# Moving one direct load of x ahead of the second group of output stores in a fused Fourier mixing and ELU kernel

## The chip, the cores and the metric

The kernel runs on one core of one Trainium2 chip. The metric is the device time of one execution in microseconds, as the median of several runs; lower is better. A profile of one execution on the same core gives the start and the duration of every instruction, the waits between engines, and the time at which DMA transfers land.

## What is computed

The input x has shape (8, 3008, 256) in float32. Each of the 8 batches goes through a two-dimensional Fourier transform, over the 3008 positions and over the 256 channels, of which the real part is kept. Each of the 24064 rows then goes through two matrices with an ELU between them:

```python
X = np.fft.fft(x, axis=1)
X = np.fft.fft(X, axis=2).real
x = X.reshape(B * S, D)
h = x @ w_in                                  # (24064, 256) @ (256, 2048)
g = np.where(h > 0.0, h, np.exp(np.minimum(h, 0.0)) - 1.0)
out = g @ w_out                               # (24064, 2048) @ (2048, 256)
```

## The kernel before

**The steady work.** Symmetry of the transform lets the kernel work on half of the positions, 8 x 1504 columns. They are cut into tiles of 256 columns, and each tile is passed over in 8 steps of two blocks of hidden units. One step is a fixed pattern on four engines. TensorE (PE) multiplies the transformed columns with the folded first matrix into the bank H (`mm_P`, `mm_Q`). VectorE (DVE) and ScalarE (ACT) make two ELU blocks of it, of which `g_plus` and `g_minus` are the last operations. GpSimd (POOL) makes four sums of blocks, in the order `sum_1`, `sum_3`, `sum_2`, `sum_4`; all of them pass through the helper at L548 and appear in the profile as `G<-G`. PE then multiplies the blocks and sums with the second matrix: `mm_X1` (L1310), `mm_X2` (L1318) and `mm_X3` (L1325). The third product of `mm_X1`, `pB<-G,WT` in the profile, reads the block that `sum_2` has written. All matmuls pass through the helper at L539.

**The output.** After a tile's 8 steps its result is combined, turned and stored. `turn_u` (L1368) transposes one half on VectorE and calls `store` twice; `turn_v` (L1389), one step later, does the same for the other half. `store` (L1398) issues its DMAs on SyncE's queue (SP) at L1424, most of them of 32 KB or less in runs of 128 bytes. Each of the two halves gives 16 or 20 stores where the change is made, and both halves go out of one buffer `ot`, of which there are two.

**The next batch.** Between these steps the kernel prepares the transform of the next batch. For batches b = 2 to 7, `load_quarter(b, j, far)` (L276) loads row tile j = 0 to 3 in two halves, near (far = 0) and far (far = 1), both into the tile `xl`j (`xq` in the profile). Tiles that are read against the order of the rows use a gather: an indirect DMA that GpSimd issues at L288. The others are direct loads on SyncE's queue at L301; a direct far half consists of two pieces, 80 rows (320 KB) and 14 rows (56 KB). For the far half, tiles 1 and 2 are direct, and 0 and 3 are gathers. `mirror_sum` (L686) then adds tile 1 to tile 0 and tile 2 to tile 3 on GpSimd, in eight parts that alternate between the two pairs, one part for each step; the first part of a pair also adds a four-element edge. `half_sum`, `channel_fold` and `channel_edge` continue from there. A far half may only be loaded when the near half in the same tile has been read to the end.

**What sets the order.** The order on PE, VectorE, ScalarE and GpSimd is written out by hand: every operation is put on a list with a due time (`at`; `rel` for the batch preparation, counted in steps of T = 4.8 from r0 = 48 b - 70), the list is sorted (L1916), and compute operations are pinned to that order. The direct loads and the stores on SyncE's queue are not pinned. The scheduler places them, so that their place in the finished program need not be their place on the list. Waits are added for data, for buffers, and for the semaphore that a DMA signals with; SyncE's DMAs take eight such semaphores (lanes) in turn, and a DMA waits until the one that had its lane before has landed.

On the list, `turn_u` of a tile stands at dt 4.2 of the step with number 3 (counted modulo 8) and `turn_v` at dt 4.2 of step 4. For a batch, step r0 + 26 is such a step 4.

Of the kernel before, what the change touches and what calls it, by code (L numbers as in the profile page):

```python
# [162 lines left out]
def kernel(  # L163
# [977 lines left out]
    def spread_ext(b, kodd):  # L1141
        for sl, a, z in ring_cut(b * HALF + kodd * RUN, RUN, False):
            a, z = a + kodd * RUN, z + kodd * RUN
            nc.sync.dma_start(
                out=Rb[:, sl],
                in_=r128_dr[b : b + 1, a:z].to_broadcast([128, z - a]),
            )
            nc.sync.dma_start(out=Ir[127:128, sl], in_=r128_dr[b : b + 1, a:z])
# [367 lines left out]
    def at(t, fn):  # L1516
        events.append((t, len(events), fn))
# [220 lines left out]
    def safe(col):  # L1738

        return 8 * ((col - 1 - RING) // TW) + 8 if col > RING else 0  # L1740
# [86 lines left out]
    def at_quarter(step, b, ri, kodd, finish, join):  # L1827
        box = []

        def d():  # L1830
            if not box:
                box.append(Quarter(ri, b, kodd, state["Q", ri, kodd, b]))
            return box[0]

        def half(par):
            d().ps = bank("H")
            d().mms(par, d().ps)

        at(step * T + 4.75, lambda: half(0))
        at((step + 1) * T + 0.9, lambda: d().copy())  # L1840
        at((step + 1) * T + 1.0, lambda: d().unfold())
        at((step + 2) * T + 4.75, lambda: half(1))
        if kodd:
            at(finish * T + 4.26, lambda: d().finish())
            at((step + 3) * T + 0.9, lambda: d().copy_odd())
            at((step + 3) * T + 1.0, lambda: d().unfold_odd())
        assert join + 1 >= safe(b * HALF + (kodd + 1) * RUN)
        t = join * T + (4.25 if kodd else 1.01)
        at(t, lambda: d().plus())
        at(t + 0.001, lambda: d().minus())  # L1850

    for b in range(2, NB):
        s0 = (b - 1) * steps_b
        r0 = 48 * b - 70

        def rel(step, dt, fn, *key):
            at((r0 + step) * T + dt, lambda: fn(*key))

        for far, rows in (
            (0, ((0, 2, 0.2), (1, 2, 1.3), (3, 3, 0.2), (2, 3, 1.3))),  # L1860
            (1, ((0, 27, 1.3), (1, 25, 0.2), (3, 28, 1.3), (2, 27, 0.2))),
        ):
            for j, n, dt in rows:
                rel(n, dt, load_quarter, b, j, far)
        rel(5, 3.0, quarter_row, b)
        for far, start in ((0, 6), (1, 30)):
            for n in range(8):
                rel(start + n, 1.3, mirror_sum, (0, 3)[n % 2], far, n // 2)
        for step, *key in (
            (13, 0, 0, 0), (20, 1, 0, 0), (21, 0, 0, 1), (22, 1, 0, 1),  # L1870
            (35, 0, 1, 0), (36, 1, 1, 0), (37, 1, 1, 1), (38, 0, 1, 1),
        ):
            rel(step, 4.25, half_sum, *key)
        for step, *key in (
            (14, 0, 0, 0), (21, 1, 0, 0), (23, 0, 0, 1), (25, 1, 0, 1),
            (38, 0, 1, 0), (40, 1, 1, 0), (42, 1, 1, 1), (44, 0, 1, 1),
        ):
            for ri in range(2):
                rel(step + ri, 1.3, channel_fold, ri, *key)
            kodd, far, h = key  # L1880
            if h:
                rel(step, 4.0, channel_edge, kodd, far)
        for n in range(4):
            ri, m = divmod(n, 2)
            rel(46 + n, 1.3, quarter_pairs, b, ri, 0, 1 + m)
        for n, step in enumerate((43, 44, 45, 46, 51, 53)):
            ri, m = divmod(n, 3)
            rel(step, 4.25, quarter_pairs, b, ri, 1, (2, 1, 3)[m])
        for step, ri, kodd, finish, join in (
            (51, 0, 0, 0, 54),  # L1890
            (56, 1, 0, 0, 59),
            (59, 0, 1, 60, 75),
            (64, 1, 1, 66, 76),
        ):
            at_quarter(r0 + step, b, ri, kodd, r0 + finish, r0 + join)
        for kodd in range(2):
            step = s0 + (28, 38)[kodd]
            assert step >= safe(b * HALF + (kodd + 1) * RUN)
            at(step * T + 1.0, lambda b=b, kodd=kodd: spread_ext(b, kodd))
# [48 lines left out]
```

## Time and profile before

| what | value |
|---|---|
| median of three timed runs | 1926.92 us (1926.02 to 1929.34) |
| the profiled execution's own time | 1925.81 us |
| its span, first to last instruction | 1924.0 us |
| granted TensorE clock | 1.000 |
| out_dram<-ot stores of 32 KB on SP | 496 |
| xq direct loads on SP: near 384 KB, far 320 KB, far 56 KB | 12 of each |
| xq gathers on GpSimd | 24, median 7.9 us from issue to landing |

Times of single instructions are microseconds from the start of the span. In the views of the profile a row of a timeline gives start, duration, engine, line, operation, tile written and tiles read, the number of merged instructions, and in brackets the engine's idle time before it with what ended that. A row of the table of waits gives the engine and line that waited, what ended the wait, the total in us, how often, and the longest. A row of the chain of waits gives start, duration, and the engine and tile that the time belongs to. A name ending in q (SPq) is the engine's queue of waits and DMA issues, which the profile doesn't count as busy.

### The profile page before, as it was taken

What the parts mean: (1) busy time and instruction counts of PE and PEld (TensorE: products, weight loads), DVE (VectorE), ACT (ScalarE), POOL (GpSimd) and SP (SyncE); (2) the same over time, 40 slices, a digit from 0 to 9 for tenths busy, and PEclk for the clock granted to TensorE, in tenths of its full rate; (3) what the DMA queues carried; (4) which work ended last, traced back from release to release, by engine and by line L of the source; (5) the groups of instructions that cost most, each with busy time, mean ns of one, the idle gap of its engine ahead of it and who ended that gap; (6) DMA issues with size and microseconds to landing.
All of it is one profiled execution on the core that took longest, in us unless ns stands there. A gap on an engine that the chain in (4) does not pass through costs nothing.

```text
span 1924.0 us, 27630 instructions
## 1 busy us (share of the span) xinstructions
PE 1910.7 (99%) x9008; PEld 1653.7 (86%) x9008; DVE 1436.7 (75%) x2714; ACT 872.7 (45%) x1710; POOL 1357.3 (71%) x1843
## 2 busy tenths in 40 slices
PE   9999999999999999999999999999999999999999
PEld 6788788888888888888888888888888888888887
DVE  8876767877777777777777777777777777667666
ACT  5644444444444444444444444444444444444443
POOL 4788857786677766787667776677766777556565
PEclk9999999999999999999999999999999999999999
DMA  8146212111021110211101111022110210100101
GB/s 337 44 34 51 45 31 55 37 23 33 12 45 36 29 31 12 51 29 32 26 19 45 33 27 27 12 52 42 26 20 12 52 23 15 17 12 13 21 11 23
DMA packets 271073, 71.88 MB, mean 37 GB/s; under 512 B 256815, under 2 KB 257731, under 8 KB 270929
## 3 DMA queue, kind: packets, MB, share of 16 engines
q1 hardware_dynamic: 257296, 57.34, 15.1%
q0 software_dynamic: 11456, 12.52, 2.2%
q8 instruction: 71, 1.16, 0.3%
q14 instruction: 74, 0.60, 0.1%
q10 hardware_dynamic: 2176, 0.26, 0.1%
HBM read 45.20 MB, written 24.80 MB: 36 GB/s over the span
## 4 chain that ended last, share of the span: by engine, by line
PE 86%; DMA 4%; POOL 3%; SPq 2%; DVE 2%; issue 1%; ACT 0%; POOLq 0%; DVEq 0%
PE H L539 34%; PE pB L539 15%; PE pC L539 15%; PE pD L539 15%; PE pA L539 7%; DMA out_dram<-ot 4%; SPq L1424 2%; POOL G L548 2%; POOL WT L548 1%; DMA xq<-in_x_dram 1%; DVE G L1223 0%; DMA xl<-in_x_dram,ix 0%; POOL e L548 0%; DVE E L1193 0%; DVE e L636 0%
## 5 line engine op out<-in xcount | busy, mean ns | idle before, releaser
L548 POOL TENSOR_TENSOR G<-G 128x256 f32<-128x256 f32 x1440 | 1046.6, 736 | 496.0 <-DVE G L1223 337.2
L551 ACT ACTIVATE G<-H 128x512 f32<-128x512 f32 x376 | 224.6, 597 | 941.3 <-DVE G L1207 936.5
L1193 DVE SCALAR_TENSOR_TENSOR E<-Rb,wex,H 128x256 f32<-128x256 f32 x752 | 327.7, 477 | 380.7 <-PE H L539 375.7
L539 PE MATMUL H<-Ir,Ws 128*128 128x256 f32 x1504 | 387.0, 380 | 2.0 <-DVE E L1193 2.0
L539 PE MATMUL H<-Rr,Wc 128*128 128x256 f32 x1504 | 387.9, 380 | 0.8 <-DVE Ir L545 0.8
L539 PE MATMUL pC<-G,WT 128*128 128x256 f32 x1440 | 369.5, 379 | 0.0
L539 PEld LDWEIGHTS H<-Ir,Ws 128*128 128x128 f32 x1504 | 278.8, 189 | 50.1 <-DVE E L1193 5.1
L539 PEld LDWEIGHTS H<-Rr,Wc 128*128 128x128 f32 x1504 | 282.1, 190 | 44.1 <-issue 2.2
L539 PEld LDWEIGHTS pC<-G,WT 128*128 128x128 f32 x1440 | 273.6, 190 | 37.2
L1207 DVE SCALAR_TENSOR_TENSOR G<-E,H 128x512 f32<-128x512 f32 x376 | 256.8, 683 | 49.5 <-POOL G L548 14.7
L1223 DVE SCALAR_TENSOR_TENSOR G<-G,H 128x512 f32<-128x512 f32 x376 | 255.8, 680 | 37.5 <-ACT G L551 37.5
L1223 DVE SCALAR_TENSOR_TENSOR G<-M,G 128x512 f32<-128x512 f32 x376 | 256.7, 683 | 0.4 <-ACT M L551 0.4
L551 ACT ACTIVATE G<-G 128x512 f32<-128x512 f32 x376 | 233.4, 621 | 0.0
L539 PE MATMUL pD<-G,w 128*128 128x256 f32 x784 | 229.3, 379 | 0.0
L539 PE MATMUL pA<-G,w 128*128 128x256 f32 x784 | 229.3, 379 | 0.0
L539 PE MATMUL pB<-G,w 128*128 128x256 f32 x784 | 229.3, 379 | 0.0
L551 ACT ACTIVATE M<-G 128x512 f32<-128x512 f32 x376 | 224.0, 596 | 3.1 <-DVE G L1207 3.1
L551 ACT ACTIVATE M<-M 128x512 f32<-128x512 f32 x376 | 221.2, 588 | 0.1
L539 PE MATMUL pB<-G,WT 128*128 128x256 f32 x720 | 215.0, 380 | 4.7 <-POOL G L548 4.6
L539 PE MATMUL pD<-G,WT 128*128 128x256 f32 x720 | 214.1, 379 | 0.0
L539 PEld LDWEIGHTS pA<-G,w 128*128 128x128 f32 x784 | 148.9, 190 | 20.5
L539 PEld LDWEIGHTS pD<-G,w 128*128 128x128 f32 x784 | 149.0, 190 | 20.3
(178 smaller groups left out, 1539.8 us busy)
## 6 DMA issues: line engine op xcount, KB each, us to landing
out_dram<-ot SPq DMA_DIRECT2D x496, 32.0 KB
xq<-in_x_dram SPq DMA_DIRECT2D x12, 384.0 KB
out_dram<-ot SPq DMA_DIRECT2D x256, 2.0 KB
xq<-in_x_dram SPq DMA_DIRECT2D x12, 320.0 KB
Rb<-r SPq DMA_DIRECT2D x10, 376.0 KB
raw<-in_moe_w_in_dram SPq DMA_DIRECT2D x7, 512.0 KB
MC<-dft_mats SPq DMA_DIRECT2D x3, 943.5 KB
xl<-in_x_dram SPq DMA_DIRECT2D x4, 512.0 KB
```

Of the source, the lines that this page charges most:

```text
L539: nc.tensor.matmul(out_, lhsT=lhsT, rhs=rhs, start=start, stop=stop, skip_group_check=True)
L548: pin(nc.gpsimd.tensor_tensor(out=o, in0=a, in1=b, op=op))
L551: pin(nc.scalar.activation(out=o, in_=i, func=func, **kw))
L1193: nc.vector.scalar_tensor_tensor(out=S.E[:, c], in0=Rb[:, cols(i)], scalar=wex[:, f : f + 1], in1=S.H[:, c], op0=ALU.mult, op1=ALU.add,)
L1207: nc.vector.scalar_tensor_tensor(out=two(S.G[:, 0:512])[:, :, ::-1], in0=two(S.E), scalar=2.0, in1=two(S.H), op0=ALU.mult, op1=ALU.subtract,)
L1223: nc.vector.scalar_tensor_tensor(out=o, in0=e, scalar=-1.0, in1=h, op0=ALU.add, op1=ALU.max)
L1424: queue.dma_start(out=bass.AP(tensor=out.tensor, offset=out.offset + r0 * ND + half * 128 + 32 * g, ap=[[2 * ND, w], [64 * ND, nb], [1, 32 ...
```

## The change

The due time of the direct load of row tile 2's far half changes from step r0 + 27, dt 0.2, to step r0 + 26, dt 3.0. On the list it then stands between `turn_u` and `turn_v` of the output tile instead of after both. Everything else is as before.

```diff
         for far, rows in (
             (0, ((0, 2, 0.2), (1, 2, 1.3), (3, 3, 0.2), (2, 3, 1.3))),
-            (1, ((0, 27, 1.3), (1, 25, 0.2), (3, 28, 1.3), (2, 27, 0.2))),
+            (1, ((0, 27, 1.3), (1, 25, 0.2), (3, 28, 1.3), (2, 26, 3.0))),
         ):
             for j, n, dt in rows:
                 rel(n, dt, load_quarter, b, j, far)
```

In each row of four the entries are the row tile j, the step and dt.

## The prediction

> **What bounds the kernel now.** I read the page's table of engines first. TensorE (PE) is busy for practically the whole span; no other engine comes near.
>
> ```profile
> PE 1910.7 (99%) x9008; PEld 1653.7 (86%) x9008; DVE 1436.7 (75%) x2714; ACT 872.7 (45%) x1710; POOL 1357.3 (71%) x1843
> ```
>
> So only a change that closes a hole in PE's row can shorten the run, and there are 1924.0 - 1910.7 = 13.3 us of holes. Next the table of waits (engine, line, what it waited for: total us, times, longest), for two rows:
>
> ```profile
> POOL xq L548 <- DMA xq<-in_x_dram: 17.4, 6, 4.4
> ...
> PE pB L539 <- POOL G L548: 4.6, 6, 1.8
> ```
>
> GpSimd (POOL) waits six times, once per batch b = 2 to 7, for a load of x; PE waits six times for GpSimd. The chain of waits that ended last joins the two. These are its steps in the second of those batches (b = 3); the columns are start, us, and who:
>
> ```profile
> 556.66 9.28 DMA out_dram<-ot
> 565.96 5.48 DMA out_dram<-ot
> 575.63 1.95 DMA xq<-in_x_dram
> 578.63 1.37 POOL G L548 x2
> ```
>
> Output stores hold up a load of x, the load holds up GpSimd, and GpSimd ends PE's wait. The same four steps return at 795.92, 1033.76, 1271.50 and 1508.99, and not in b = 2. Now each engine's own timeline at that place. SyncE's queue (SP):
>
> ```profile
> 541.49 9.03 SPq L301 DMA_DIRECT2D xq<-in_x_dram  x3
> 550.63 24.95 SPq L1424 DMA_DIRECT2D out_dram<-ot  x40
> 575.63 0.33 SPq L301 DMA_DIRECT2D xq<-in_x_dram  x1
> 576.05 0.35 SPq L1144 DMA_DIRECT2D Rb<-r  x1
> ```
>
> Of the four pieces of direct load (two each for row tiles 1 and 2), three are issued by 550.5. The last, the 14-row piece of tile 2 (56 KB), stands behind all 40 stores of one output tile: 20 of turn_u, 20 of turn_v. GpSimd:
>
> ```profile
> 568.62 0.89 POOL L548 TENSOR_TENSOR xq<-xq,xq 94x255 f32<-94x255 f32 x2
> 570.31 3.03 POOL L548 TENSOR_TENSOR G<-G 128x256 f32<-128x256 f32 x4 [0.79 <-DVE G L1223]
> 577.73 0.90 POOL L548 TENSOR_TENSOR xq<-xq,xq 94x255 f32<-94x255 f32 x2 [4.40 <-DMA xq<-in_x_dram]
> 578.57 3.03 POOL L548 TENSOR_TENSOR G<-G 128x256 f32<-128x256 f32 x4
> ```
>
> The second mirror_sum of the far half could have begun at 577.73 - 4.40 = 573.33. The four G<-G behind it are sum_1, sum_3, sum_2 and sum_4; sum_2, the third, ends near 580.8. PE:
>
> ```profile
> 578.42 0.59 PE L539 MATMUL pB<-G,w 128*128 128x256 f32 x2
> 580.85 0.70 PE L539 MATMUL pB<-G,WT 128*128 128x256 f32 x2 [1.83 <-POOL G L548]
> 581.38 0.81 PE L539 MATMUL H<-Ir,Ws 128*128 128x256 f32 x3
> ```
>
> The matmul that stalls is the third product of mm_X1, which reads the block that sum_2 writes.
>
> **What the Trainium skill says.** (1) "DMA: Bandwidth & Descriptors", section "Anatomy of one DMA": DMA engines do not wait on semaphores; the issuing sequencer does, before dispatch. The trace agrees: SP issues nothing between 560.8 and 562.9, nor between 563.2 and 566.0, while an earlier store on its semaphore lane is still landing (lanes are used eight in turn, so a ninth DMA waits for the first). (2) The same page, "Queues, rings and completion order": on each DMA engine the descriptors of one issuing queue are consumed in ring order. The trace agrees as far as it can: the load that follows the drained stores lands in 1.95 us, while stores issued into the backlog need 4.7 to 9.7 us. (3) The same page, "Issuing engines are not separate DMA queues": SP's transfers and GpSimd's gathers run on the same 16 engines and interleave. The two gathers of b = 3 take 12.2 and 11.5 us beside the stores, against a median of 7.9 for all 24.
>
> **The change, part by part.** It removes and adds no instruction. The two programs as built have the same order on PE, VectorE, ScalarE and GpSimd. On SP the 80-row piece stays where it was, ahead of all the stores; only the 14-row piece moves, from behind turn_v's stores to between turn_u's and turn_v's: 20 stores sooner (16 in b = 2). The waits on readers of the tile stay with the 80-row piece; the 14-row piece keeps one wait, for its semaphore lane. The lanes of the stores it passes shift by one. The gathers' place on GpSimd's queue is unchanged, and so is what follows on SP (the Rb and Ir spreads at 576.05).
>
> When does the 14-row piece land now? It takes the place and the lane of turn_v's first store, so I use that store's times. In b = 3 it was issued at 560.50, and its lane was taken again at 569.12, so it had landed by then. In the other batches: b = 2 321.94 and 329.77; b = 4 799.20 and 807.01; b = 5 1036.71 and 1045.31; b = 6 1273.56 and 1281.96; b = 7 1510.97 and 1518.79. GpSimd's earliest need (start of the waiting mirror_sum less its wait) is 336.65, 573.33, 812.09, 1049.91, 1287.17 and 1525.08. The margins are 6.9, 4.2, 5.1, 4.6, 5.2 and 6.3 us. The wait for this piece should disappear in every batch.
>
> What is late next? The same mirror_sum waits for the gather of tile 3. The gathers land at 334.59, 571.20, 809.50, 1046.84, 1284.54 and 1522.49, which is 2.1 to 3.1 us ahead of need. There is also a cover between GpSimd and PE: GpSimd waited 4.40, 3.48, 2.92, 3.16 and 3.18 us in b = 3 to 7, and PE stood for 1.83, 0.92, 0.34, 0.60 and 0.61. The difference is 2.56 to 2.58 us each time. A GpSimd wait under 2.57 us costs PE nothing, and b = 2 confirms it: 0.27 us of wait and no stall. So the gather could come some 4.7 us later than now before PE noticed.
>
> Could the moved piece delay a gather so much? Its 14 packets of 4 KB take about 0.26 us each, and they go to 14 engines. That puts 0 to 0.3 us ahead of other traffic, against 4.7 us of cover: cost nothing. turn_v's stores go out one place later, by 0.3 us (the issue time of one such DMA) up to the 2.4 us that SP may wait for the next lane (562.91 - 560.50), but the sum of issues ahead of the Rb spread is unchanged, and it was issued on VectorE's release at 576.11. The output buffer that these stores read is wanted again two tiles, or 16 steps of about 4.75 us, later. That slack of over 70 us hides it.
>
> What is a stall worth? PE's start-to-start distance is what is lost, and it is more than the idle time printed, because a matmul's modelled end lies after the next one's start. From the start of mm_X1's pB<-G,w to the start of the next H<-Ir,Ws, b = 2, which has no stall, takes 337.86 - 336.99 = 0.87 us. In b = 3 it takes 581.38 - 578.42 = 2.96, so 2.09 is lost. In b = 4 to 7 the distances are 2.06, 1.47, 1.73 and 1.74, so 1.19, 0.60, 0.86 and 0.87. The sum is 2.09 + 1.19 + 0.60 + 0.86 + 0.87 = 5.61 us. The printed idle times alone give 1.83 + 0.92 + 0.34 + 0.60 + 0.61 = 4.30 us: that is the lower bound. Between 337 and 1525 the table of stages shows PE busy to the full in every stretch without such a stall, so no other wait is in line behind them, and b = 2 shows the next 48 steps running on without one. I take 5.6.
>
> The span falls from 1924.0 to 1918.4. The profiled execution took 1925.81 us, 1.81 more than its span; the same on top gives 1920.2. The three timed runs have a median of 1926.92, 1.1 above the profiled one. On that median: 1926.92 - 5.6 = 1921.3.
>
> **The rivals.** *Part of it* (chance 0.08): the piece lands later than turn_v's first store did, since a 4 KB packet in a ring of 128 B ones need not behave the same, or the gather moves later, so that some wait beyond the cover stays. For it: SP's backlog is worst just there. Against: over 4 us of margin and 2.57 of cover. With half of the loss left, 1926.9 - 2.8 = 1924.1.
>
> *Nothing* (0.05): the wait closes and PE loses the time to another engine later, for instance because VectorE used the stall to catch up. Against: VectorE is at 75%, and after the stall-free b = 2 PE is full from 337 to 574. It would give 1926.9.
>
> *Slower* (0.04): the gather becomes the last to land and is pushed back by the earlier piece. It must come later than the 14-row piece did before (577.58, 815.41, 1052.67, 1290.17, 1528.10), so by 5.6 to 6.4 us; from there every us costs one per batch. If gathers were 8 us later they would end 2.4 to 3.4 us past need plus cover in each of six batches, 17.5 us in all: 1926.9 + 17.5 - 5.6 = 1938.8. For it: they share the engines. Against: 0.3 us of traffic.
>
> **How the numbers follow.** The full gain has 0.83. A measurement here can tell about 0.2%, or 3.85 us, from no change, so the bound is 1923.07. Faster: 0.82 of the full gain and 0.03 of the partial one; slower 0.04; the rest is the same. The range: downwards 5.6 plus 0.4 (a small PE loss between 1295 and 1525 which might go too) below the fastest run, 1926.02, hence 1919.5 with a little for scatter; upwards past the lower bound (1922.6) to the partial case at 1924.2.
>
> **What would show it.** Right: GpSimd's row of waits on xq falls from 17.4 us to under 2; the row PE pB on POOL G loses its five stalls; the chain passes no out_dram or xq step; SP issues a single xq load between two groups of 20 stores near 560. Wrong: the mirror_sum still waits near its present length, with a gather as the one that ended it; or PE shows a new releaser within some steps of the old stall.

## The result, and the profile after

The changed kernel takes 1921.05 us (median of six runs, 1920.68 to 1921.22), beside 1927.99 us for the kernel before (six runs, 1926.02 to 1931.73). The ratio is 0.9962, with a 95% interval of 0.9949 to 0.9975: faster by 0.25 to 0.5%. The forecast was 1921.3, in a range of 1919.5 to 1924.2. The profiled execution of the changed kernel took 1921.02 us with a span of 1919.1, against 1925.81 and 1924.0.

First SyncE's queue in batch b = 3, at the place shown in the prediction:

```profile
542.04 9.04 SPq L301 DMA_DIRECT2D xq<-in_x_dram  x3
551.20 9.03 SPq L1424 DMA_DIRECT2D out_dram<-ot  x20
561.00 0.34 SPq L301 DMA_DIRECT2D xq<-in_x_dram  x1
563.54 13.05 SPq L1424 DMA_DIRECT2D out_dram<-ot  x20
576.69 0.35 SPq L1144 DMA_DIRECT2D Rb<-r  x1
```

The single load, the 14-row piece, now stands between two groups of 20 stores. It was issued at 561.00 instead of 575.63, and the last signal of its landing came at 567.47 (its lane was taken again at 568.74). The second group of stores begins later (563.54; it was 560.50), and the Rb spread only 0.64 us later, both counted from the start of the span. Of each, 0.5 us was there before this place was reached: the same steps at 436 already run that much later in this execution.

GpSimd at the same place:

```profile
569.17 0.89 POOL L548 TENSOR_TENSOR xq<-xq,xq 94x255 f32<-94x255 f32 x2
570.88 3.02 POOL L548 TENSOR_TENSOR G<-G 128x256 f32<-128x256 f32 x4 [0.82 <-DVE G L1223]
573.86 0.89 POOL L548 TENSOR_TENSOR xq<-xq,xq 94x255 f32<-94x255 f32 x2
576.21 3.03 POOL L548 TENSOR_TENSOR G<-G 128x256 f32<-128x256 f32 x4 [1.46 <-PE H L539]
```

The second mirror_sum follows the sums without a bracket, that is, without a wait. GpSimd then waits for the ordinary step of the pattern. PE:

```profile
578.99 0.59 PE L539 MATMUL pB<-G,w 128*128 128x256 f32 x2
579.42 0.59 PE L539 MATMUL pB<-G,WT 128*128 128x256 f32 x2
579.86 1.03 PE L539 MATMUL H<-Ir,Ws 128*128 128x256 f32 x4
```

From pB<-G,w to H<-Ir,Ws it is 579.86 - 578.99 = 0.87 us, the undisturbed distance; it was 2.96. The table of waits has no row of GpSimd on the direct load any more (it was 17.4 us, 6 times), and of the row of PE pB on POOL G (4.6 us, 6 times) this is left:

```profile
PE pB L539 <- POOL G L548: 0.3, 1, 0.3
```

That one wait, at 226.6, lies ahead of these batches and was there before too (226.2); the five stalls are gone. The chain that ended last has no store and no load of xq in it. By engines it reads, before and after:

```profile
PE 86%; DMA 4%; POOL 3%; SPq 2%; DVE 2%; issue 1%; ACT 0%; POOLq 0%; DVEq 0%
```

```profile
PE 96%; DVE 1%; POOL 1%; ACT 0%; DMA 0%; issue 0%; DVEq 0%; POOLq 0%
```

### The profile page after: what moved, and what is told of

It reads as the page before. It is cut to its first block, busy times and chain, and to the rows that moved or that the text cites. A ratio compares the mean times of both kernels' runs of the same rounds, so it can differ in the third digit from the quotient of the medians.

```text
span 1919.1 us, 27636 instructions
## 1 busy us (share of the span) xinstructions
PE 1909.2 (99%) x9008; PEld 1653.4 (86%) x9008; DVE 1436.9 (75%) x2714; ACT 872.3 (45%) x1710; POOL 1356.9 (71%) x1843
## 4 chain that ended last, share of the span: by engine, by line
PE 96%; DVE 1%; POOL 1%; ACT 0%; DMA 0%; issue 0%; DVEq 0%; POOLq 0%
PE H L539 38%; PE pB L539 17%; PE pC L539 17%; PE pD L539 16%; PE pA L539 9%; POOL WT L548 1%; DMA xl<-in_x_dram,ix 0%; POOL w L548 0%; DVE e L636 0%; ACT G L551 0%; DVE pow L407 0%; DVE o L636 0%; DVE E L1193 0%; DVE G L1223 0%; DVE G L1207 0%
## 5 line engine op out<-in xcount | busy, mean ns | idle before, releaser
L548 POOL TENSOR_TENSOR G<-G 128x256 f32<-128x256 f32 x1440 | 1045.6, 735 | 508.6 <-DVE G L1223 341.9
```

Source lines behind the costliest of these rows:

```text
L548: pin(nc.gpsimd.tensor_tensor(out=o, in0=a, in1=b, op=op))
```

## The experiments

The theory: the 14-row piece lands late because of its place behind the stores, GpSimd waits for it, and what goes beyond 2.57 us of that wait becomes a stall of PE. The main rivals: every store ahead of the load costs its share; the due time or the kind of load is what counts; the gather is the next bound. "Before" and "after" are the two kernels of the change. Each run was timed beside the kernel before, on the same chip.

| run | median us | ratio to before, 95% interval | GpSimd waits for xq, us (b = 2 to 7) | PE idle in the stalls, us |
|---|---|---|---|---|
| before, first profile | 1926.92 | | 0.27, 4.40, 3.48, 2.92, 3.16, 3.18 | 0, 1.83, 0.92, 0.34, 0.60, 0.61 |
| e0, before again | 1927.68 | 1.0002 (0.9993 to 1.001) | 0.54, 4.56, 4.11, 3.51, 3.49, 3.09 | 0, 1.99, 1.54, 0.96, 0.92, 0.53 |
| after | 1921.05 | 0.9962 (0.9949 to 0.9975) | none | none |
| e1, big piece last | 1937.67 | 1.0051 (1.0037 to 1.0065) | 0.62, 5.26, 5.25, 4.88, 5.48, 3.89 | 0, 2.68, 2.67, 2.30, 2.90, 1.31 |
| e2, behind 8 stores of turn_v | 1921.12 | 0.9967 (0.9954 to 0.9979) | none | none |
| e3, behind 12 | 1920.55 | 0.9964 (0.9951 to 0.9978) | 0, 0, 0.63, 0.44, 0.32, 0 | none |
| e4, one piece | 1921.66 | 0.9968 (0.9955 to 0.998) | none | none |
| e5, gather one step later | 1921.53 | 0.997 (0.9959 to 0.9981) | 1.87, 2.43, 2.83, 2.38, 2.15, 2.14 | 0, 0, 0.27, 0, 0, 0 |
| e6, gather two steps later | 1963.53 | 1.0184 (1.017 to 1.0198) | 7.55, 6.16, 6.31, 5.78, 6.12, 7.57 | 5.75, 4.36, 4.51, 4.00, 4.34, 5.86 |

**The kernel before, once more (e0).** No edit.

> The kernel before, unchanged, for a second profile and more times. My theory (the small load lands late, GpSimd waits, and what exceeds 2.57 us of that wait becomes a PE stall): five PE stalls again at pB<-G,WT, each equal to GpSimd's wait on xq less 2.57 us; if this execution is slower than the first profiled one (1925.81 us), the stalls are longer by just that, since the landing of the load is what varies. Rival (the runs of before vary for another reason, in the front or at the end): stalls as in the first profile, the difference elsewhere.

The second profiled execution took 1927.56 us, 1.75 more than the first. Its table of waits has:

```profile
POOL xq L548 <- DMA xq<-in_x_dram: 19.3, 6, 4.6
...
PE pB L539 <- POOL G L548: 6.3, 6, 2.0
```

GpSimd waits 1.9 us more than the first time, and PE's waits in the same row are 1.7 us longer (6.3 against 4.6). PE's idle time is again the wait less 2.55 to 2.57 in each batch with a stall. So the longer time of this execution lies in the stalls, as the theory has it, and not in the front or at the end.

**The big piece behind the stores (e1).** The two pieces change places:

```diff
-        for p, q in ((0, 80), (80, 94)) if far else ((0, 96),):
+        for p, q in ((80, 94), (0, 80)) if far and j == 2 else ((0, 80), (80, 94)) if far else ((0, 96),):
```

> The two pieces of tile 2's far half change places: the 14-row piece goes ahead of the stores and the 80-row piece (320 KB) stands behind them all. Theory (position decides, not the amount of work or the due time): it is issued when the small one was, near 575.6 in b = 3, and needs about 1 us more to land (its packets took some 1.6 us longer at 551 to 553), so each GpSimd wait grows by about 1 us to 4.0 to 5.5, each of the five stalls by the same, and b = 2 stays under the cover of 2.57. Some 5 us over the kernel before, 1932 to 1934. Rival (any 56 KB piece in the backlog was the trouble, a big load is quicker because it goes over all engines): no slower than before, 1921 to 1928.

The waits came out close to the forecast of 4.0 to 5.5 (3.89 to 5.48), and b = 2 stayed under the cover. GpSimd in b = 3:

```profile
579.63 0.89 POOL L548 TENSOR_TENSOR xq<-xq,xq 94x255 f32<-94x255 f32 x2 [5.26 <-DMA xq<-in_x_dram]
```

But the time was 1937.7, not 1932 to 1934. One cause shows in PE's row:

```profile
582.74 1.22 PE L539 MATMUL pB<-G,WT 128*128 128x256 f32 x2 [2.68 <-POOL G L548]
583.75 1.91 PE L539 MATMUL H<-Ir,Ws 128*128 128x256 f32 x4
```

Four matmuls that take 1.03 us elsewhere take 1.91. The table of stages (from:to, length, then busy time and instructions of PE, PEld, DVE, ACT and POOL, then granted clock, DMA share, GB/s) tells why:

```profile
575.00:580.00 5.00, 5.00 (x24) 4.09 (x22) 4.29 (x8) 3.42 (x7) 0.37 (x1) 1.00 0.55 146
580.00:585.00 5.00, 2.32 (x6) 1.85 (x6) 2.23 (x5) 0.00 (x0) 4.84 (x9) 0.73 0.01 2
585.00:590.00 5.00, 5.00 (x23) 4.36 (x22) 2.76 (x5) 2.12 (x4) 3.51 (x6) 0.92 0.01 2
```

The granted clock falls to half, from 582.3 to 585.8, behind the stall, and again from 824.7 to 828.1. Summed over the distances from one matmul's start to the next, beyond the 0.216 us of steady work, the five stalls lose 12.67 us, and the matmuls right behind them another 3.67, of which 3.15 is the halved clock. The sum of 16.3 agrees with the difference of the spans of e1 and after, 1935.9 - 1919.1 = 16.8. My 5 us were for the longer stalls alone; they are 12.7 - 6.8 = 5.9 us more than in e0, and with the clock's 3.15 on top of e0's 1927.7 one comes to 1936.7, 1 us short of the median. The rival, no slower than before, is out: it is the place behind the stores that costs, whichever piece stands there.

**Behind 8 of turn_v's stores (e2).** In after, `load_quarter` keeps the 14-row piece of tile 2 back, and `turn_v` issues it:

```diff
         store(q, 2, 0, 0)
+        if "late" in state:
+            state.pop("late")()
         store(q, 3, 1, 1)
```

> After, but the 14-row piece behind the first 8 of turn_v's stores. Theory: issued near 569 in b = 3, it lands within 4 to 5 us, at or just past need (573.9); GpSimd waits 0 to 1 us, inside the cover of 2.57, and PE has no stall: 1921.0, as after. Rival (the gain goes with the place, each store ahead costs its share): 8 of 20 stores give back about two fifths of the gain of 6.9 us, 1923.8.

No wait and no stall; the whole gain stays. In b = 3 the piece was issued at 569.03 and had landed at 572.65. The place is worth nothing by itself, as long as the piece lands in time.

**Behind 12 of them (e3).** The same hold-back, with the issue inside `store`, after the first four DMAs of part 3:

```diff
+                if part == 3 and "late" in state:
+                    state.pop("late")()
                 at_ += w * nb
```

> After, but the 14-row piece behind 12 of turn_v's stores (8 or fewer follow it). Theory: issued near 572 in b = 3, it lands near 575; GpSimd waits 0.5 to 2.2 us in most batches, the table of waits shows again 4 to 10 us on xq in total, and still PE has no stall, or one of under 0.3 us: 1921 to 1921.5. Rival (a wait of GpSimd passes on to PE in proportion): three fifths of the gain given back, 1925.

The time held and the size of the waits did not: 1.4 us in three batches, where I had expected 4 to 10. The piece landed faster than I assumed, in 2.0 us in b = 4 (809.13 to 811.17), and in 2.1 us in b = 3 (571.95 to 574.02), about as fast as behind all the stores in the kernel before (1.95 us). GpSimd in b = 4 (lines of this kernel's own numbering; L555 is the helper at L548):

```profile
811.33 0.89 POOL L555 TENSOR_TENSOR xq<-xq,xq 94x255 f32<-94x255 f32 x2 [0.63 <-DMA xq<-in_x_dram]
```

PE shows nothing near it. The rival of a share for each store, 1925, is out.

**One DMA in place of two (e4).** In before, with the old due time:

```diff
-        for p, q in ((0, 80), (80, 94)) if far else ((0, 96),):
+        for p, q in ((0, 94),) if far and j == 2 else ((0, 80), (80, 94)) if far else ((0, 96),):
```

> The kernel before with tile 2's far half loaded by one DMA of 94 rows instead of 80 + 14, at the old due time; as built it stands ahead of all the stores. Theory (only the piece that was left behind the stores made the stall): no GpSimd wait on xq and no PE stall, 1921 to 1922, if the one DMA lands by 573 in b = 3; a 94-row load may go over few DMA engines and take long, which would show as stores that land later and, past 576, as stalls. Rival (the due time on the list is what helps): as before, 1927.

The gain is there with the due time untouched, because the scheduler put the one DMA ahead of the stores (issued at 550.66 in b = 3). So the due time matters only through the place that the scheduler gives the second piece. The load of 376 KB kept its lane until 560.1, 9.4 us, where the 80-row load of 320 KB in before was off its lane within 3.7 us (550.20 to 553.89). The Trainium skill, "DMA: Bandwidth & Descriptors", section "Why a DMA increments its semaphore by 16 and not by 1", says that a DMA is spread over the largest number of engines up to 16 that divides the outer dimension of both sides: 16 for 80 rows and 2 for 94. The trace agrees: after the first signal, which comes at the issue, the landing of the 94 rows has two, at 560.07 and 560.09, and that of the 80 rows has 16, from 552.93 to 553.49. That is a reason for the split. The 40 stores took until 579.68 instead of 575.58, and nothing waited for that.

**The gather one and two steps later (e5, e6).** After, with tile 3's gather moved:

```diff
-            (1, ((0, 27, 1.3), (1, 25, 0.2), (3, 28, 1.3), (2, 26, 3.0))),
+            (1, ((0, 27, 1.3), (1, 25, 0.2), (3, 29, 1.3), (2, 26, 3.0))),
```

and with 30 in place of 29.

> After, with the gather of tile 3's far half one step (4.75 us) later on GpSimd. The prediction put the gather's room at 2.1 to 3.1 us ahead of need plus the cover of 2.57. Theory: it lands up to 2.6 us past need, GpSimd waits 0.5 to 2.6 us per batch for it, PE stalls by nothing or under 0.3 us: 1921 to 1922. Rival (the gather has no such room and is the next bound): each batch gives back 2 us or more, 1930 and over.

> After, with the same gather two steps (9.5 us) later. Theory: it lands 3 to 7 us past need (less of the store backlog is left by then, so it takes 8 to 11 us instead of 11.3), GpSimd waits so long, and PE stalls in all six batches by the wait less 2.57 us plus some 0.27: 0.7 to 4.7 us each, 1925 to 1946. Rival (GpSimd has more room than the cover says, or the lateness is caught up): under 1923.

In e5 GpSimd waits about 2 us in every batch, and PE stands in one only. In b = 3, and PE in b = 4:

```profile
576.09 0.89 POOL L548 TENSOR_TENSOR xq<-xq,xq 94x255 f32<-94x255 f32 x2 [2.43 <-DMA xq<-in_x_dram,ix]
```

```profile
816.47 0.70 PE L539 MATMUL pB<-G,WT 128*128 128x256 f32 x2 [0.27 <-POOL G L548]
```

b = 4 is the batch whose wait was 2.83, and 2.83 - 2.57 = 0.26. (The profile puts that wait down to VectorE, whose update came at 813.30; the gather had landed at 813.28.) This is the sharpest test of the cover: 2.43 us of waiting is free, 2.83 costs 0.27.

In e6 the direction was right and the size not: 1963.5 instead of at most 1946. GpSimd in b = 3:

```profile
577.72 1.49 POOL L288 DMA_INDIRECT xq<-in_x_dram,ix  x1 [0.17 <-issue]
579.24 0.89 POOL L548 TENSOR_TENSOR xq<-xq,xq 94x255 f32<-94x255 f32 x2
580.08 3.01 POOL L548 TENSOR_TENSOR G<-G 128x256 f32<-128x256 f32 x4
589.25 0.89 POOL L548 TENSOR_TENSOR xq<-xq,xq 94x255 f32<-94x255 f32 x2 [6.16 <-DMA xq<-in_x_dram,ix]
```

The gather took as long as ever, 11.5 us (577.72 to 589.18); I had expected it to be faster past the stores. Its issue now stands next to a mirror_sum, 1.49 and 0.89 us in one step, so that GpSimd itself comes later and the cover falls to 6.16 - 4.36 = 1.80 us. And at each of the six stalls, from its last part or just behind it, the clock is halved for 3.4 or 6.8 us. The stalls lose 29.8 us from start to start and the matmuls behind them 13.5, together 43.3; the spans differ by 1962.3 - 1919.1 = 43.2. I had left out the clock and the smaller cover.

## Why the prediction was right, step by step

**Place and landing: right.** As run, the 14-row piece moved by 20 stores (16 in b = 2), and all six waits for it were gone. The bound from the store whose place it took (landed within 8.6 us in b = 3) held with room: the piece took 6.5 us there, 4.9 in b = 2 and 6.3 to 6.9 in b = 4 to 7. That is longer than the 1.95 us of before, so what the change gains is the earlier issue, 14.6 us, and not a quicker transfer.

**The gather: unchanged, as costed.** In b = 3 it lands 11.5 us after its issue, before (559.67 to 571.20) and after (560.25 to 571.74). The room of some 4.7 us that I gave it is borne out by e5, where 4.75 us more is absorbed in all batches but one, and by e6, where 9.5 us is not. The slower rival was thus a real mechanism that this change doesn't set off.

**The cover of 2.57 us: right** for the order of this kernel, and tested on both sides by e5, and by e0 and e1 above it. In e6, where GpSimd has more to do in that step, it was 1.80 us in b = 3: it belongs to the order and not to the wait.

**The size: right for the profiled execution.** The same step of the pattern stands at 435.57 and 1624.88 in before and at 436.05 and 1619.91 in after: 1189.31 against 1183.86, a gain of 5.45 us where I had 5.61. The difference is about what PE now loses in small gaps between 436 and 812, 0.2 us by the starts of its matmuls. The span fell by 4.9 because this execution was 0.48 us later ahead of that stretch. This also settles which measure of a stall is right: the idle time printed gave 4.30, the distance of starts 5.61.

**The median: right with some luck.** It fell by 6.9, not 5.6. By the same sum from start to start e0 loses 7.3 us and the first profile 5.65, so the one execution I had seems to be one with short stalls; the clock may have a part too (last section). My base of three runs (1926.92) was a us low, and the two errors nearly cancel. The time after is what the stalls don't touch.

## What to carry to other kernels

Look at which piece of a load lands last and at its place on the queue, not at the due time of the load in the source: a 56 KB piece behind 40 stores held up a multiply engine that was busy 99% of the time. Work out the cover between a wait and the bound engine from several instances of the same wait (here wait less stall was 2.57 us five times over); it tells how early is early enough, and where the next load may go. Take the price of a stall from starts of the bound engine's instructions, not from the idle time printed.

## What the runs showed of the hardware

A stall of PE can cost more than its length. In e1 two of the stalls (idle 2.68 and 2.67 us) were followed by 3.4 us of granted clock 0.5, while those of 2.90, 2.30 and 1.31 were not; in e6 all six (4.0 to 5.9 us) had it, for 3.4 or 6.8 us. The Trainium skill, "TensorE: Matmul & The Clock Gate", section "What's actually happening", tells of a clock gate that halves the clock after an idle window of about 3.4 us, which runs freely; the length of the slow stretches agrees.

Which stalls are hit can be read from the traces, and it is not the length alone. All changes of the clock that one trace records lie on a grid of 3.413 us: in e1 the slow stretches are 582.34 to 585.75 and 824.68 to 828.10, and their starts are 71 such windows apart. I laid this grid over the 22 stalls in the traces of before, e0, e1, e5 and e6. The eight that left PE idle for 2.27 us or more of one window got half clock from the end of that window; the other 14, with at most 1.99 us in any one window, did not. The 2.90 us in e1 got away because the grid cuts them into 0.95 and 1.94. The slow stretch went on for a second window in the three cases where PE was idle for another 0.69 to 1.89 us of the first one, and not where that was 0.40 or nothing. So here less than a full idle window was enough, and where the grid happens to stand decides whether a stall like those in e1 costs some 1.6 us more.

A late DMA also seems to make the time vary. The kernel before ran from 1924.97 to 1932.36 us in the 18 runs beside e0 to e3, after from 1920.68 to 1921.22, and e2 and e4, which have no wait either, within 0.6 us; e3 and e5, with waits under the cover or just past it, spread over 1.8 and 1.9 us. The two profiles of before differ in their stalls by nearly the difference of their times, so part of the scatter seems to be that of the landing; it was seen in two executions only. The clock seems to be another part. In 16 of the 43 executions of before (e0 and those beside e0 to e6) the mean granted clock is 0.999 instead of 1.000, and the ten slowest are all among them; the median is 1929.3 us for the 16 and 1927.1 for the rest. In after and e2 to e5 it is 0.999 in one of 30. One window at half clock costs PE 1.7 us, or 0.0009 of the mean, so this fits a stall that now and then halves the clock. None of the 16 was profiled, so that is not shown.
